# One more unit's second product by two Strassen levels, the second group's experts reordered, and w2 operands made in the first five units

## The chip, the core and the metric

The kernel runs on one core of a Trainium2 chip. The metric is the device time of one execution in microseconds (us). Three executions of the kernel before took 1161.64, 1163.95 and 1164.05 us; their median is 1163.95 us. Everything is float32.

## What is computed

The reference is a blockwise linear attention followed by a mixture of four expert networks. Cut to what matters here:

```python
# q, k, v: (4, 8, 768, 64) -> attn_out of the same shape, by blocks of 64 rows
x = attn_out.transpose(0, 2, 1, 3).reshape(3072, 512)      # 3072 tokens
p = probs / (probs.sum(-1, keepdims=True) + 1e-9)          # (3072, 4)
for e in range(4):
    h = np.maximum(x @ w1[e], 0.0)                         # first product, 512 -> 1024
    out += p[:, e:e + 1] * (h @ w2[e])                     # second product, 1024 -> 512
```

## The kernel before

**Units.** The 3072 tokens are cut into three groups of 1024, and a unit is one group with one expert: `units` (line 122) lists twelve of them. Group 0 takes the experts in the order 0, 1, 2, 3, group 1 likewise, and group 2 (`LAST`) in the order 2, 3, 0, 1. The main loop (line 1631) has an iteration `at` for each unit. In iteration `at` TensorE (PE) does the second product of unit `at` and, woven between, the first product of unit `at + 1`. An iteration has seven steps `i`, one for each of the seven Strassen products of the outer level, and each step has eight slots `x`; there are thus 56 slots in an iteration. `now[0]` counts slots, and all planning on the host side is done in slots. The program is written out in full from this plan, so the order on each engine is fixed when the kernel is built.

**Products.** The first product of all units but the first runs by two Strassen levels (`first_product`, line 993; matmuls at line 1017): 7 x 7 small products of two matmuls each. Its weights come ready made from DRAM: for each outer product a tile `ws_in` of 896 KB (`feed`, line 927, DMA at line 930), one step before it is used, into two buffers. The second product runs in one of two ways. In units before `NEST` = 6 it has one Strassen level (`second_product`, line 1056; matmuls at 1071, q<-w2t,m in the profile): seven products of 4 x 4 matmuls. In units from `NEST` on it has two levels (`nested_product`, line 1350; matmuls at 1370, pq): 7 x 7 products of two matmuls. A matmul of 128x128 weights with 256 columns is two MATMUL records in the profile, so a step of a plain unit has 28 + 32 records and a step of a nested unit 28 + 28.

**What a nested unit needs besides.** The gates are multiplied into the hidden layer before the product (`gated`, line 857: 16 multiplications of 128x512 on POOL), outer sums of it are made on VectorE (DVE) with copies into PSUM by ScalarE (ACT) (`outer_sums`), inner sums on POOL (`inner_sums`, 28 subtractions of 128x512), and results are added up in seven tiles `sums[m]` (transposed) that are allocated from the `stage` buffers at unit `NEST`. Results of a group's plain units are added up in `acc` tiles instead. Group 1 has both: the plain part is written to DRAM (`partial`) at unit `NEST - 1` and added to the nested part in unit 8 and after (`first_result`).

**Weights of the nested units.** They are ready-made operands too (`w2_ops` in DRAM): `prepare_w2_ops(e, eased)` (line 317) loads w2 of an expert by eight DMAs, makes four totals (eight operations of 128x512) and, in `inner_w2` (line 306), for each of the seven outer products four sums of 128x256, all on POOL, and stores them by six DMAs a product, 42 for an expert (line 315). With `eased` its tiles are from the pool of 42 `small` tiles, otherwise from the seven `stage` buffers. Experts 2 and 3 are made from unit 4 on and experts 0 and 1 from unit 6 on (`PREPARED`, line 1630). `prepare_w1(e)` makes the first product's operands the same way, by four loads and three stores a product, 21 for an expert (lines 218 to 220); `prepare_w2(e)` the sums for the one-level product.

**Chores.** These preparations are lists of small steps in `chores`. `pump` (line 185) is called once a slot and starts the next chore when the planned time of the one before is over: a chore's POOL time in slots, times `PACE` (1.0 in group 0, 1.4 in group 1), and at least 7 slots once `spare` is set at unit `NEST`. Stores are put off (`store`) until the planned end of the sums. `until(what)` runs chores at once until `what` is made.

**Attention of the later groups.** Groups 1 and 2 get their attention while the units before run. `BEGIN` (line 794) gives the slot of a group's first chunk of 128 tokens and the spacing of the eight chunks: (24, 13) for group 1, (152, 16) for group 2. A chunk's loads go out 10 and 6 slots ahead. Group 2 reads q and k in a transposed order that 128 small DMAs of 32 KB, DRAM to DRAM, bring about first (`bring_across`, line 435, DMAs at 441); `trickle` issues them one by one, in every second slot (`if x % 2`, line 1717), and `load_more` issues at once what a chunk still lacks.

**Queues.** Nearly every DMA is issued by SyncE (SP), in program order: `ws_in`, the small ones, attention's loads, the stores of chores. An instruction that waits there holds back all that follow. PE, DVE, ACT and POOL are in order as well.

Of the kernel before, what the change touches and what calls it, by code (L numbers as in the profile page):

```python
# [21 lines left out]
def kernel(  # L22
# [33 lines left out]
    E, DM, F = moe_w1.shape  # L56
# [6 lines left out]
    CPG = 8  # L63
    G = CPG * C
    NG = NTOK // G
# [23 lines left out]
    def bank(tag, name):  # L89
        return ps.tile([P, W], FP32, name=name, tag=tag)  # L90
# [28 lines left out]


    LAST = NG - 1
    units = [(g, e) for g in range(NG) for e in ((2, 3, 0, 1) if g == LAST else range(E))]
    unit_of = {u: x for x, u in enumerate(units)}
    NEST = 2 * E - 2
    FINAL = len(units) - 1

    def token(g, half, x):
# [45 lines left out]
    chores, queue, late, results, made = [], [], [], [], set()  # L173
# [32 lines left out]
    def until(what):  # L206
        while what not in made:
            pump(force=True)
# [582 lines left out]
        ))  # L791

    FILL = {1: 18, 2: 43}
    BEGIN = {1: (24, 13), 2: (8 * 19, 16)}
    steps = []

    def attention(g):
# [258 lines left out]
    def second_product(g, e, m, banks):  # L1056

        def part(sj, s):
            i, j = ADD[m]
            t = f"q{sj}" + ("1" if m in ("M1", "M6", "M5", "M3") else "2")  # L1060
            fresh = m in ("M1", "M2", "M7")
            if fresh and s == 0:
                banks[t] = bank(t, t)
            p = banks[t]
            first = True
            for uu in range(2):
                h = hid[g, e, uu, sj]
                while A_OF[m] not in h:
                    rest(force=True)
                for c in range(2):  # L1070
                    nc.tensor.matmul(  # L1071
                        out=p[:, s * DH:(s + 1) * DH],
                        lhsT=h[A_OF[m]][:, c * 256 + s * P:c * 256 + (s + 1) * P],
                        rhs=fed2[g, e, m][uu][:, c], start=(fresh and s == 0 and first), stop=True,
                        skip_group_check=True,
                    )
                    first = False
            n = g * CPG + sj * 4 + i * 2 + s
            if n not in acc:
                acc[n] = acc_tile("acc"), set()  # L1080
            a, begun = acc[n]
            o, x, w = a[:, j * DH:(j + 1) * DH], p[:, s * DH:(s + 1) * DH], gate[:, n, e:e + 1]
            if e == 0 and j not in begun:
                vector(DH, True)
                nc.vector.tensor_scalar(out=o, in0=x, scalar1=w, scalar2=None, op0=ALU.mult)
                begun.add(j)
            else:
                vector(DH, True)
                nc.vector.scalar_tensor_tensor(out=o, in0=x, scalar=w, in1=o, op0=ALU.mult, op1=ALU.add)  # L1089
            if unit_of[g, e] in (E - 1, NEST - 1) and m in ("M2", "M6", "M5", "M3"):  # L1090
                to = rows[n] if g == 0 else partial[n % CPG * P:(n % CPG + 1) * P]
                results.append(lambda: nc.sync.dma_start(out=to[:, j * DH:(j + 1) * DH], in_=o))

        def done():
            del fed2[g, e, m]
            if m in ("M4", "M5", "M3"):
                for uu in range(2):
                    for sj in range(2):
                        del hid[g, e, uu, sj][A_OF[m]]

        return [lambda sj=sj, s=s: part(sj, s) for s in range(2) for sj in (1, 0)] + [done]


# [523 lines left out]
        attention(g)  # L1627
    PACE = 1.0, 1.4, 1.0
    first_steps = first_result()
    PREPARED = {NEST - 2: (2, 3), NEST: (0, 1)}  # L1630
    for at, (g, e) in enumerate(units):
        if at == 0:
            chores.extend(prepare_w2(2) + prepare_w1(3) + prepare_w2(3) + prepare_w1(0))
        ahead = units[at + 1] if at + 1 < len(units) else None
        nested, nests = at >= NEST, ahead and at + 1 >= NEST
        if at in PREPARED:
            for x in PREPARED[at]:
                chores.extend(prepare_w2_ops(x, nested))
        if at == NEST:
            spare.append(True)  # L1640
        if at == NEST - 1:
            forget()
        blocks, banks = {}, {}
        for i in range(7):
            if fill2:
                feed2(*fill2.pop(0))
            if not nested:
                later_operands(g, e, SEQ2[i])
            if nested or (nests and i == 6):
                for _ in range(2 if ahead else 16 if i == 0 else 4 if i > 1 else 0):  # L1650
                    if fill3:
                        feed3(*fill3.pop(0))
            if nests and i == 2:
                nc.scalar.dma_start(
                    out=gate_bc, in_=gate_rows[ahead[0] - 1, :, ahead[1]].partition_broadcast(P),
                )
            if nested:
                pair = (at * 7 + i) % 2 if ahead else i % 3
                b = nested_product(at, SEQ3[i], (("q01", "q02"), ("q11", "q12"), ("g1", "g3"))[pair])
                if i < 6 and (at, SEQ3[i + 1]) != PLAIN:  # L1660
                    inner_sums(at, SEQ3[i + 1])
            else:
                b = second_product(g, e, SEQ2[i], banks)
            if nests and i == 6:
                inner_sums(at + 1, SEQ3[0], nested)
                if at + 1 == EARLY[0]:
                    inner_sums(*EARLY, True)
            a = []
            if ahead:
                a = first_product(*ahead, SEQ[i], blocks, ("g1", "g3"))  # L1670
            if nested and (at, SEQ3[i]) == END:
                b[6:6] = [lambda: (give("M4", 1, ("s0", "s1"), (1,)), turn_end(1, "q11"))]
                b[5:5] = [lambda: (give("M4", 0, ("s0", "s1"), (1,)), turn_end(0, "q12"))]
            if not ahead:
                order = [[], b[0:2], [], b[2:4], [], b[4:6], [], b[6:]]
            elif nested:
                order = [b[0:2], a[0:2], b[2:4], a[2:4], b[4:6], a[4:6], b[6:8], a[6:8]]
            else:
                order = [b[0:1], a[0:2], b[1:2], a[2:4], b[2:3], a[4:6], b[3:5], a[6:8]]
            turned_back = list(after_last.get(SEQ3[i], ())) if nested and not ahead else []  # L1680
            for x, part in enumerate(order):
                for f in part:
                    if f:
                        f()
                now[0] += 1
                if (at - 2 * E + 1, i, x) in first_steps:
                    first_steps.pop((at - 2 * E + 1, i, x))()
                if joins:
                    joined()
                elif (ahead or x % 2 == 0 and x + i) and not (nests and i == 6 and x == 7):  # L1690
                    if nested or nests:
                        rest()
                    else:
                        took = False
                        for of in (lately, background, own_sums):
                            if of and (not took or fits() or of is background and len(of) > 1):
                                take(of)
                                took = True
                if nested or nests:
                    take(aside)  # L1700
                    if own_sums and fits():
                        take(own_sums)
                if ending and fits():
                    end_first()
                if nested and ahead and x in (1, 3) and fill3:
                    feed3(*fill3.pop(0))
                if turned_back and x > 0:
                    for y in turned_back.pop(0):
                        if SEQ3[i] == END[1]:
                            give(*y[:2], ("s0", "s1"), *y[2:])  # L1710
                        else:
                            give_across(*y)
                if x == (4 if nested else 0) and at * 7 + i >= 6 and fill:
                    feed(*fill.pop(0))
                while steps and (at * 7 + i) * 8 + x == steps[0][0]:
                    steps.pop(0)[1]()
                if x % 2:
                    trickle()
                for h in range(1, NG):
                    if x == 3 and 0 <= at * 7 + i - FILL[h] < 7:  # L1720
                        x_fill(h, SEQ[at * 7 + i - FILL[h]])
                pump(PACE[g])
# [30 lines left out]
```

## Time and profile before

| what | value |
|---|---|
| median of three runs | 1163.95 us (1161.64 to 1164.05) |
| profiled execution, first to last instruction | 1164.6 us (no other time is given for it) |
| PE busy with matmuls | 1149.6 us, 99% |
| DVE, POOL, ACT busy | 810.8, 748.3, 306.2 us (70%, 64%, 26%) |
| matmuls L1017 pg (first product) | 1960 records, 472.0 us |
| matmuls L1071 q (second product, one level) | 1344 records, 318.7 us |
| matmuls L1370 pq<-acc,w2t (second product, two levels, the largest of its groups) | 576 records, 141.9 us |
| DMA | 270.63 MB, mean 232 GB/s |

The iterations of the main loop begin at these times, read from the first matmul of line 1017 that belongs to each: 92, 193, 299, 397, 497, 596, 688, 773, 858, 946 and 1030 us; the last one, at = 11, begins at about 1115 us. Before 92 us lie group 0's attention and its first unit's first product. A view by windows gives the busy time of each engine between two times, with the number of records in brackets, the granted TensorE clock (1.00 is full), the mean busy share of the 16 DMA engines and what they moved. The chain of waits lists what ended last, followed back from the end: a start, a length, the engine and the group it was in, and how many records.

### The profile page before, as it was taken

Reading aid. Unit: us, or ns where it says so; the run is one execution under the profiler, and the core shown is the slowest. Engines: PE = TensorE matmul, PEld = TensorE weight load, DVE = VectorE, ACT = ScalarE, POOL = GpSimd, SP = SyncE. Lnnn points to the kernel's source line nnn. Section 1 sums busy time; section 2 is a strip of 40 time slices with the busy share of each in tenths; the row PEclk is TensorE's granted clock in tenths of the full one; section 3 lists DMA queues with packets and bytes.
Section 4 is the critical chain, followed back from the end, with each engine's and each line's share of the span. In section 5 each row is a group of like instructions: output and inputs, shape, how many; then the busy total and the mean of one; then the engine's idle time right before and its main releaser. Section 6 shows DMA issues by size and latency. Waiting matters only on the chain.

```text
span 1164.6 us, 21683 instructions
## 1 busy us (share of the span) xinstructions
PE 1149.6 (99%) x8039; PEld 997.4 (86%) x8039; DVE 810.8 (70%) x1483; ACT 306.2 (26%) x618; POOL 748.3 (64%) x720
## 2 busy tenths in 40 slices
PE   8899999999999999999999999999999999999998
PEld 7788888888888888888888888888888888888887
DVE  4576896477478757747946775688875677777785
ACT  4312122112201211221221243342343341341232
POOL 2747427456754862243646395897995898995894
PEclk9999999999999999999999999999999999999999
DMA  8883668999999797787969557676668877876542
GB/s 191 213 277 119 182 190 255 311 297 284 314 301 298 258 315 204 205 261 240 291 204 281 187 190 227 213 225 216 212 222 261 244 230 227 277 225 212 172 190 73
DMA packets 291705, 270.63 MB, mean 232 GB/s; under 512 B 139600, under 2 KB 239504, under 8 KB 291600
## 3 DMA queue, kind: packets, MB, share of 16 engines
q1 hardware_dynamic: 278848, 265.36, 74.1%
q10 hardware_dynamic: 12752, 3.89, 1.5%
q8 instruction: 64, 1.05, 0.4%
q14 instruction: 41, 0.34, 0.1%
HBM read 191.55 MB, written 81.82 MB: 235 GB/s over the span
## 4 chain that ended last, share of the span: by engine, by line
PE 93%; DVE 4%; DMA 1%; issue 1%; ACT 0%; ACTq 0%; DVEq 0%
PE pg L1017 39%; PE q L1071 24%; PE pq L1370 19%; PE pM L1473 3%; PE pc L1473 2%; DVE m L102 2%; PE sp L676 1%; PE op L730 1%; DMA ws_in<-w_ops 1%; PE op L748 1%; PE sp L683 1%; DVE sums L102 1%; PE qp L646 1%; PE kp L646 1%; DVE hT L102 0%
## 5 line engine op out<-in xcount | busy, mean ns | idle before, releaser
L1017 PE MATMUL pg<-xs,ws_in 128*128 128x256 f32 x1960 | 472.0, 381 | 2.3 <-DMA ws_in<-w_ops 1.2
L1017 PEld LDWEIGHTS pg<-xs,ws_in 128*128 128x128 f32 x1960 | 369.5, 190 | 56.5 <-DVE m L102 4.6
L102 DVE TENSOR_TENSOR m<-pg,m 128x512 f32<-128x512 f32 x451 | 307.1, 687 | 124.6 <-PE pg L1017 112.8
L1071 PE MATMUL q<-w2t,m 128*128 128x256 f32 x1344 | 318.7, 380 | 0.5 <-DVE m L102 0.5
L1071 PEld LDWEIGHTS q<-w2t,m 128*128 128x128 f32 x1344 | 254.1, 190 | 35.8 <-DVE m L102 1.2
L102 POOL TENSOR_TENSOR m<-m,decay 128x512 f32<-128x512 f32 x96 | 121.0, 1282 | 75.2 <-ACT m L1029 58.0
L1029 ACT ACTIVATE m<-m 128x512 f32<-128x512 f32 x132 | 83.0, 630 | 244.4 <-DVE m L102 241.0
L1370 PE MATMUL pq<-acc,w2t 128*128 128x256 f32 x576 | 141.9, 379 | 0.2 <-DVE sums L102 0.2
L102 DVE TENSOR_TENSOR sums<-pq,sums 128x256 f32<-128x256 f32 x223 | 92.7, 421 | 59.2 <-PE pq L1370 47.8
L1089 DVE SCALAR_TENSOR_TENSOR acc<-q,gate,acc 128x256 f32<-128x256 f32 x136 | 65.4, 481 | 87.5 <-PE q L1071 86.6
L1370 PEld LDWEIGHTS pq<-acc,w2t 128*128 128x128 f32 x576 | 109.2, 190 | 15.7 <-POOL w2o L102 0.5
L102 DVE TENSOR_TENSOR m<-m,m 128x512 f32<-128x512 f32 x136 | 112.9, 830 | 4.2 <-ACT m L1029 4.2
L1025 ACT COPY m<-pg 128x512 f32<-128x512 f32 x88 | 51.5, 585 | 161.7 <-PE pg L1017 158.7
L102 POOL TENSOR_TENSOR acc<-hT,acc 128x512 f32<-128x512 f32 x48 | 61.3, 1276 | 5.2 <-PE pq L1370 1.8
L102 POOL TENSOR_TENSOR to<-xc 128x256 f32<-128x256 f32 x16 | 12.6, 785 | 79.6 <-DVE xc L102 47.1
L102 POOL TENSOR_TENSOR acc<-hT,hT 128x512 f32<-128x512 f32 x48 | 60.7, 1282 | 3.9 <-PE pq L1370 3.9
L1370 PE MATMUL pq<-hT,w2t 128*128 128x256 f32 x240 | 61.6, 379 | 0.0
L102 POOL TENSOR_TENSOR xs<-xs 128x256 f32<-128x256 f32 x40 | 30.4, 761 | 47.0 <-DMA xs<-x_blocks 33.3
L102 POOL TENSOR_TENSOR kn<-kn,decay 128x512 f32<-128x512 f32 x16 | 18.1, 1133 | 63.2 <-PE kp L646 27.6
L949 ACT COPY up<-m 128x512 f32<-128x512 f32 x48 | 27.8, 589 | 101.6 <-DVE m L102 101.4
L881 ACT COPY hp<-m 128x512 f32<-128x512 f32 x72 | 41.6, 589 | 37.5 <-DVE hT L102 20.3
L1370 PEld LDWEIGHTS pq<-hT,w2t 128*128 128x128 f32 x240 | 45.6, 190 | 6.2
(140 smaller groups left out, 1371.0 us busy)
## 6 DMA issues: line engine op xcount, KB each, us to landing
ws_in<-w_ops SPq DMA_DIRECT2D x70, 896.0 KB, 6.9
w2t<-w_ops SPq DMA_DIRECT2D x108, 256.0 KB, 3.7
w2b<-in_moe_w_dram SPq DMA_DIRECT2D x56, 256.0 KB, 6.1
w_ops<-ops SPq DMA_DIRECT2D x28, 512.0 KB, 4.7
w2t<-w_sums SPq DMA_DIRECT2D x48, 256.0 KB, 3.7
w2t<-in_moe_w_dram SPq DMA_DIRECT2D x36, 256.0 KB, 3.9
w_sums<-w2o SPq DMA_DIRECT2D x16, 512.0 KB, 5.4
xs<-x_blocks SPq DMA_DIRECT2D x28, 256.0 KB, 4.5
```

The costliest lines, as they stand in the source:

```text
L102: eng.tensor_tensor(out=o, in0=a, in1=b, op=op)
L646: nc.tensor.transpose(out=x[:, ac * C:(ac + 1) * C], in_=y[:, 2 * ac:2 * ac + 2].rearrange("p r d -> p (r d)"), identity=ident[:],)
L676: nc.tensor.matmul(out=sp[r][half[x], ac * BL:(ac + 1) * BL], lhsT=hc(kT)[half[r], ac, blk[x]], rhs=hc(qT)[half[r], ac, blk[x]], start=(ac ...
L881: nc.scalar.copy(out=there[x][:], in_=blk[at][:])
L949: nc.scalar.copy(out=there[at][:], in_=a[at][:])
L1017: nc.tensor.matmul(out=p[:, j * 256:(j + 1) * 256], lhsT=ws[i][:, j * P:(j + 1) * P], rhs=xs[i], start=(fresh and j == 0), stop=True, skip ...
L1025: nc.scalar.copy(out=new[at][:], in_=p[:])
L1029: nc.scalar.activation(out=new[at][:], in_=new[at][:], func=AF.Relu)
L1071: nc.tensor.matmul(out=p[:, s * DH:(s + 1) * DH], lhsT=h[A_OF[m]][:, c * 256 + s * P:c * 256 + (s + 1) * P], rhs=fed2[g, e, m][uu][:, c], ...
L1089: nc.vector.scalar_tensor_tensor(out=o, in0=x, scalar=w, in1=o, op0=ALU.mult, op1=ALU.add)
L1370: nc.tensor.matmul(out=p[:, 0:256], lhsT=fed3[e, m, x // 2][:, x % 2, c * P:(c + 1) * P], rhs=b[B_OF[i]][:, c * 256:(c + 1) * 256], start= ...
L1473: nc.tensor.matmul(out=p[:, s * 256:(s + 1) * 256], lhsT=a[c][:, f:f + P], rhs=b[:, c, j * 256:(j + 1) * 256], start=(s == 0 and c == 0 an ...
```

## The change

The unit before the nested ones becomes nested too (`NEST` is 5). Group 1 takes its experts in the order 1, 2, 3, 0, so that its one plain unit is expert 1, and expert 0's first-product operands are needed at unit 7 instead of unit 4. The w2 operands of experts 2 and 3 go into the chores ahead of expert 0's w1 operands, those of expert 0 after them, all from unit 0 on; only expert 1's are left for unit `NEST`, which begins by running chores until expert 0's w1 operands are made. Attention of group 1 is spaced by 12 slots instead of 13; that of group 2 begins at slot 24 + 12 * 8 = 120 instead of 152, spaced by 12 instead of 16, so that it ends before unit 4. The small DMAs go out in every slot instead of every second one from step 8 on (the second step of unit 1).

```diff
-    units = [(g, e) for g in range(NG) for e in ((2, 3, 0, 1) if g == LAST else range(E))]
+    ORDER = {0: (0, 1, 2, 3), 1: (1, 2, 3, 0), LAST: (2, 3, 0, 1)}
+    units = [(g, e) for g in range(NG) for e in ORDER[g]]
...
-    NEST = 2 * E - 2
+    NEST = 2 * E - 3
...
-    BEGIN = {1: (24, 13), 2: (8 * 19, 16)}
+    BEGIN = {1: (24, 12), 2: (24 + 12 * CPG, 12)}
...
-            if e == 0 and j not in begun:
+            if e == ORDER[g][0] and j not in begun:
...
-    PREPARED = {NEST - 2: (2, 3), NEST: (0, 1)}
     for at, (g, e) in enumerate(units):
         if at == 0:
-            chores.extend(prepare_w2(2) + prepare_w1(3) + prepare_w2(3) + prepare_w1(0))
+            chores.extend(prepare_w2(2) + prepare_w1(3) + prepare_w2(3))
+            for x in (2, 3):
+                chores.extend(prepare_w2_ops(x, False))
+            chores.extend(prepare_w1(0))
+            chores.extend(prepare_w2_ops(0, True))
...
-        if at in PREPARED:
-            for x in PREPARED[at]:
-                chores.extend(prepare_w2_ops(x, nested))
         if at == NEST:
+            until(("w1", 0, "M4"))
+            chores.extend(prepare_w2_ops(1, True))
             spare.append(True)
...
-                if x % 2:
+                if x % 2 or at * 7 + i >= 8:
                     trickle()
```

## The prediction

> **What bounds the kernel now.** First the busy shares, then the chain of waits, then the stages by windows, then SP's timeline. The page and its chain:
>
> ```profile
> PEclk9999999999999999999999999999999999999999
> DMA  8883668999999797787969557676668877876542
> ...
> PE 93%; DVE 4%; DMA 1%; issue 1%; ACT 0%; ACTq 0%; DVEq 0%
> ```
>
> PE at full clock is the chain for 93%, in every slice. DMA is near full in slices 7 to 14 (about 200 to 440 us) and lower after. The chain, step by step inside unit 6, shows the price of a matmul record:
>
> ```profile
> 698.58 1.73 PE pq L1370 x8
> 700.31 1.73 PE pg L1017 x8
> 702.03 1.73 PE pq L1370 x8
> ```
>
> Eight records take 1.73 us, 0.216 us each, in both products; the 381 ns of the groups' list are overlapping records. One step of a plain and one of a nested iteration, by windows (two records more are counted than start inside):
>
> ```profile
> 609.40:622.35 12.95, 12.95 (x62) 11.40 (x61) 4.01 (x7) 2.34 (x4) 4.28 (x5) 1.00 0.95 279
> 700.15:712.24 12.09, 12.09 (x58) 10.64 (x57) 5.65 (x10) 5.72 (x12) 7.94 (x8) 1.00 0.66 199
> ```
>
> 60 records last 12.95 us, 56 last 12.09 us, PE without a gap in both. So PE bounds iterations 1 to 10, and what counts is records removed and gaps added.
>
> **Removed: matmuls.** Unit 5's second product changes from 7 x 32 = 224 records to 7 x 28 = 196. 28 x 0.216 = 6.05 us; by the steps, 7 x (12.95 - 12.09) = 6.02 us. I take **-6.0**. All of it is on the path. Attention's matmuls are moved, not changed, and cost the same wherever they lie.
>
> **Added beside PE in unit 5 and just before.** POOL: 16 gate multiplications x 1.282 + 28 inner sums x about 1.28 = 56 us; one more gate broadcast of 512 KB. DVE: 49 additions x 0.421 + 16 outer sums x 0.68 = 31.5 us in place of 28 x 0.481 + 16 x 0.83 = 26.8 us, +5 us. ACT: 20 copies into PSUM x 0.589 = 12 us. The cover is what the iterations that are nested already show, with the same work:
>
> ```profile
> 688.00:773.00 85.00, 84.93 (x394) 74.24 (x392) 55.16 (x92) 33.65 (x73) 65.97 (x60) 1.00 0.73 232
> 773.00:858.00 85.00, 84.98 (x393) 74.58 (x394) 71.83 (x131) 27.56 (x49) 74.24 (x68) 1.00 0.71 224
> ```
>
> POOL is busy 66 and 74 of 85 us and PE loses 0.1. There POOL carried w2 operands too, which partly leave. I cost it at 0; were the cover gone, each POOL operation that a matmul waits for costs 1.28 us. The 1 us gap on the way into nesting (670 us, PE waits for two DVE additions) moves to the unit before and stays.
>
> **Moved: w2 operands.** One expert is 8 totals x 1.39 + 28 sums x 0.77 = 32.7 us of POOL, 8 loads and 42 stores. Experts 2 and 3 move from 503 to 653 us to about 350 to 490 us, directly where expert 0's w1 operands (until 426 us now) end; those follow until about 570 us, then expert 0's w2. POOL has room: 58 of 98 us in unit 2, 44 of 100 in unit 3. In slots: an expert's w2 or w1 is planned at 11 x 2.13 + 8 = 31 slots; w1 of expert 0 now ends at slot 184 (426 us); in its place stands expert 2's w2, then 31 for expert 3's w2 and 6 for sums of x that come earlier, to 221, then 31 x 1.4 = 43 for w1, to 264. The forced run at slot 280 (596 us, as now) finds it made, with 16 slots to spare; what it costs if not is a rival. The seven `sums` tiles then take stage buffers that are free. In units 6 to 9 the w2 work falls from two experts to one and a rest: less POOL, less on SP. Unit 9's start now has 3.1 us of gaps (86.18 us of PE in 88 between 858 and 946, the step at 883.6 waiting for a ws_in of 11.68 us, issued behind stores, `parked` and w2 loads). Part may go; DVE's backlog there, and SP's waits on `sums`, stay. Between 0 and -3.1, I take **-0.5**, as only four of SP's entries just ahead of that ws_in are w2 loads.
>
> **Moved: attention of group 2 and the small DMAs.** This is where the room is smallest. The four stages from unit 1 on:
>
> ```profile
> 193.00:299.00 106.00, 105.92 (x1030) 91.44 (x1028) 71.53 (x130) 21.91 (x48) 63.99 (x68) 1.00 0.93 288
> 299.00:397.00 98.00, 97.45 (x697) 84.43 (x689) 66.51 (x113) 18.20 (x38) 58.47 (x62) 1.00 0.95 301
> 397.00:497.00 100.00, 100.00 (x839) 86.47 (x838) 68.97 (x125) 17.09 (x36) 43.55 (x53) 1.00 0.80 240
> 497.00:596.00 99.00, 99.00 (x835) 85.80 (x834) 69.59 (x124) 17.67 (x40) 46.83 (x54) 1.00 0.86 262
> ```
>
> The share of the DMA engines is 0.93 and 0.95 exactly where work is put. SP's timeline for these stages has 119, 109, 109 and 107 DMAs that keep SP 87, 79, 66 and 74 us. How near the next weights are to being late shows in unit 1: the DMA below goes out 11.8 us ahead of its first matmul, and needs 6.9 us in the median.
>
> ```profile
> 226.91 0.53 SPq L930 DMA_DIRECT2D ws_in<-w_ops  x1
> ```
> ```profile
> 238.74 1.99 PE L1017 MATMUL pg<-xs,ws_in 128*128 128x256 f32 x8
> ```
>
> So some 4 to 5 us are left there; in unit 2, with SP less behind, the same DMA goes out a full step ahead (7 to 9 us left). What the change adds:
>
> Unit 1: 36 small DMAs are out by 193 us, then 29, 29 and 34 a unit. With 4 + 6 x 8 they become 52 in unit 1, 40 in unit 2, none in unit 3: +23, +11, -34. A small one keeps SP 0.6 us (its median), 0.95 in unit 1 (27.7 us for 29). With 4 loads for group 2's first chunk, unit 1 gets 27 more: 17 us at the median, 87 + 17 = 104 of 106 us. SP no longer catches up there.
>
> Unit 2: +11 small ones, three more chunks of group 2 with 11 loads, 11 stores and 4 loads for w2 in place of w1, 3 stores of x: +40 DMAs x 0.6 = 24 us, 79 + 24 = 103. A chunk's matmuls take 2.2 us in the chain (L676 0.62, L683 0.47, L730 0.62, L748 0.47), so three of them lengthen the unit to some 105. Full again. Unit 3: -34 small ones, but 50 for w2 and 3 for x more: +19, at 66 us. Unit 4 gets emptier.
>
> The gap that this makes isn't in the trace, so from both sides. Below: 0; PE waited 1.2 us for ws_in in all, and DMA engines bear more than 0.95 for a step (1.07 between 425 and 440 us, PE 15.00 of 15). Above: at 0.95 us for each entry in unit 1, and 0.73 (79 / 109) in unit 2, with 6 us between entries, 119 and 114 us of SP are wanted in 106 and 105; less the 5 us that ws_in has left, 8 + 9 = 17 us of PE waiting. I take **+2**, nearer the lower end, since unit 2's own rows (0.95, no gap) are the nearest to the new state, and 0.6 a median.
>
> The rule that speaks against it is in the Trainium skill, DMA: Bandwidth & Descriptors, section Bandwidth: transfers under 64 KB are mostly descriptor cost. Our rows agree: 32 KB land in 4.6 us, 256 KB of w2t in 3.7. The fit that the page gives in its section on the anatomy of one DMA (2.0 us + bytes / 436e3, estimate 2.1 us for 32 KB) would leave the small ones harmless: 0 in place of +2, and a sum of -6.0. By the rule, with the upper bound, the sum would be +11. The measured 4.6 stands between.
>
> DVE in unit 2 carries three chunks more, about 5 us each on 66.5 us of 98, and is ahead of PE only in bursts (2.7 us of DVE stand in the chain at 377 us, where PE lost 0.9). Between 0 and three such gaps, 2.7 us; I take **+0.5**.
>
> **Sum.** -6.0 - 0.5 + 2 + 0.5 = -4.0, against the profiled span of 1164.6: 1160.6. The page gives no time beyond the span; the span lies 0.65 above the median of the runs, 1163.95, so I put the same difference on the median: **1160.0 us**.
>
> **Rivals.** (a) *SP overfull, slower than before.* Small DMAs and w2 stores put ws_in behind its step in units 1 to 3; each late one stops PE and what is lost doesn't come back. For it: the 11.8 us above, 0.95 share, 0.95 us a small DMA. Against: no gap yet from this cause there, slack in units 3 and 4. It decides from 6.5 us of waiting on (6.0 + 0.5); at 9 to 17 us the time is 1166 to 1175, say 1169. (b) *The same, smaller:* 4 to 8 us of waiting eat the gain, 1162 to 1166, say 1163.5. (c) *Relief is fuller:* no new gaps and unit 9's 3.1 us gone, -9.1: 1154.9. (d) *The change doesn't do what it says:* chores lag, and the forced run at unit 5 pours expert 0's w1 operands on POOL ahead of the gates. Three products are 12 sums x 0.77 = 9 us, the last iteration's outer sums wait: -4 + 9, 1169.
>
> **Chances.** Forecast 0.45 (1157.5 to 1161.6), (c) 0.07, (b) 0.18, (a) 0.24, (d) 0.06. This kernel's measurement can tell 0.2% (2.3 us) from no change. Forecast and (c) are faster: 0.52; (b) within: 0.18; (a) and (d) slower: 0.30. The range leaves out half of (c) and the upper part of (a): 1156 to 1171; the forecast's own range is 1157.5 to 1161.6.
>
> **What would show it.** L1071 at 1344 - 224 = 1120 records, L1370's groups 196 more; steps of 12.09 us from unit 5 on. Unit 5's iteration 85 us, not 92. For +2: ws_in going out 10 to 12 us before its step through unit 2, PE's waits for it below 4 us in all. If units 1 to 3 are longer by more than 6.5 us over their moved attention, (a) holds. If POOL is full around 596 us and PE waits at the first steps of unit 5, (d). If unit 5's steps are not 12.09, the cover on POOL failed.

## The result and the profile after

The changed kernel takes 1190.92 us (median of four runs, 1185.02 to 1194.33), the kernel before beside it 1163.34 us. The ratio on record, which is not the quotient of these two medians (1.0237), is 1.0227 with a 95% interval of 1.0201 to 1.0253. Of all executions in this document one, of the kernel with the small DMAs at full rate in unit 0, took 4034.55 us; it is left out of that kernel's ratio. Forecast were 1160.0 us, with a range of 1156 to 1171. The profiled execution took 1193.83 us and spans 1192.0 us, 27.4 us more than the span of before. Where the program says L1017, L1071, L1370, L930 and L441 for the kernel before, the kernel after has L1018, L1072, L1371, L931 and L442.

First the page of after, its DMA row of the 40 slices and its chain of waits:

```profile
DMA  8884667889899999979786767686686967566642
...
PE 78%; DMA 8%; POOL 6%; DVE 5%; issue 2%; SPq 1%; ACT 1%; ACTq 0%; POOLq 0%; DVEq 0%
```

PE's share of the chain fell from 93% to 78%; 8% of it is DMA now. The slices are too coarse to place that, the windows are not. The first column after the stretch is its length, the second PE's busy time; the last three are the clock, the DMA share and GB/s. Here are iterations 1, 2 and 5 of after:

```profile
194.00:311.00 117.00, 110.28 (x1102) 94.32 (x1100) 73.53 (x133) 23.87 (x54) 60.38 (x65) 0.99 0.87 260
311.00:431.00 120.00, 108.12 (x960) 91.19 (x964) 74.81 (x132) 17.86 (x40) 61.84 (x68) 0.96 0.93 279
...
629.00:714.00 85.00, 84.79 (x393) 74.40 (x392) 50.91 (x88) 34.21 (x72) 70.81 (x65) 1.00 0.72 219
```

Unit 5 (629 to 714 us) is what the change was to make of it: 85 us in place of 92, with 0.2 us of gaps. Units 1 and 2 are 117 and 120 us long where they were 106 and 98; PE idles 6.7 and 11.9 us in them, and the granted clock is 0.99 and 0.96. The share of the DMA engines is 0.87 and 0.93 there, and was 0.93 and 0.95 before: it fell while PE stood, which speaks against the engines being short. The first experiment tests that. The groups of the page of after say for what PE waits (the last column):

```profile
L1018 PE MATMUL pg<-xs,ws_in 128*128 128x256 f32 x1960 | 479.5, 385 | 21.7 <-DMA ws_in<-w_ops 18.8
L1072 PE MATMUL q<-w2t,m 128*128 128x256 f32 x1120 | 267.0, 381 | 0.5 <-DVE m L102 0.5
```

And its waits between 194 and 431 us, with the sum, the number and the longest:

```profile
PE pg L1018 <- DMA ws_in<-w_ops: 16.3, 8, 4.4
```

PE waits 18.8 us for `ws_in` in the whole run (1.2 before), 16.3 us of them in eight waits in units 1 and 2. One of these steps in the chain of waits of after:

```profile
335.80 0.29 SPq L1053
...
336.18 7.50 DMA ws_in<-w_ops
...
343.82 3.61 PE pg L1018 x8
347.43 1.73 PE q L1072 x8
```

The step before began at 326.9 us, and with it the buffer came free. SP issued the DMA at 336.18, 9.3 us later; it landed after 7.50 us, and PE's step began 16.9 us after the last one. Why SP came late stands on its own timeline of after, just ahead:

```profile
328.14 0.90 SPq L219 DMA_DIRECT2D w_ops<-w1o  x1
...
330.14 1.50 SPq L442 DMA_DIRECT2D across<-in_k_dram  x2
331.69 1.28 SPq L442 DMA_DIRECT2D across<-in_q_dram  x2
333.01 0.60 SPq L219 DMA_DIRECT2D w_ops<-w1b  x1
...
334.69 1.40 SPq L1053 DMA_DIRECT2D w2t<-w_sums  x2
336.18 0.44 SPq L931 DMA_DIRECT2D ws_in<-w_ops  x1
```

Between these entries lie 0.05 to 0.1 us: SP goes from one to the next and is behind, with six stores of operands, four small DMAs and two loads ahead of `ws_in`. The transfer itself is hardly slower: from issue to landing `ws_in` takes 6.9 us in the median of either kernel, and 7.4 in unit 2 of after (6.5 before).

**The account.** The loss of an iteration is its length, from first matmul to first matmul, less its records at the price of a step without gaps (0.216 us each, attention's matmuls at the times of the prediction), so it holds what slow clock costs as well:

| iteration | 0 | 1 | 2 | 3 | 4 | 5 | 6 | 7 | 8 | 9, 10 | sum |
|---|---|---|---|---|---|---|---|---|---|---|---|
| before, us | 1.7 | 0.6 | 1.1 | 0.6 | 0.5 | 1.1 | 0.4 | 0.2 | 3.2 | 0.2 | 9.5 |
| after, us | 3.9 | 10.0 | 18.4 | 1.7 | 5.8 | 0.1 | 1.8 | 1.0 | 2.2 | 0.2 | 44.9 |

35.4 us more loss, 6.0 us fewer matmuls and an iteration 0 that begins 1.2 us earlier (90.7 us) make 28.2; measured are 27.4, and 0.8 us stays unplaced. Units 1 and 2 carry 26.7 of it.

### The profile page after: what moved, and what is told of

Same layout as the page of the kernel before. It is cut to its first block, busy times and chain, and to the rows that moved or that the text cites. A ratio compares the mean times of both kernels' runs of the same rounds, so it can differ in the third digit from the quotient of the medians.

```text
span 1192.0 us, 21838 instructions
## 1 busy us (share of the span) xinstructions
PE 1155.0 (97%) x8011; PEld 996.4 (84%) x8011; DVE 821.9 (69%) x1504; ACT 316.6 (27%) x638; POOL 802.9 (67%) x764
## 4 chain that ended last, share of the span: by engine, by line
PE 78%; DMA 8%; POOL 6%; DVE 5%; issue 2%; SPq 1%; ACT 1%; ACTq 0%; POOLq 0%; DVEq 0%
PE pg L1018 33%; PE pq L1371 20%; PE q L1072 15%; DMA ws_in<-w_ops 6%; POOL acc L102 2%; PE pM L1474 2%; POOL m L102 2%; PE pc L1474 2%; DVE m L102 2%; DVE sums L102 1%; DVE xs L102 1%; PE op L731 1%; PE sp L677 1%; POOL ops L102 1%; PE op L749 1%
## 5 line engine op out<-in xcount | busy, mean ns | idle before, releaser
L1018 PE MATMUL pg<-xs,ws_in 128*128 128x256 f32 x1960 | 479.5, 385 | 21.7 <-DMA ws_in<-w_ops 18.8
L1018 PEld LDWEIGHTS pg<-xs,ws_in 128*128 128x128 f32 x1960 | 371.6, 192 | 80.8 <-issue 15.7
L1072 PE MATMUL q<-w2t,m 128*128 128x256 f32 x1120 | 267.0, 381 | 0.5 <-DVE m L102 0.5
L1072 PEld LDWEIGHTS q<-w2t,m 128*128 128x128 f32 x1120 | 214.4, 192 | 31.1 <-DVE m L102 1.2
L102 POOL TENSOR_TENSOR m<-m,decay 128x512 f32<-128x512 f32 x112 | 141.2, 1279 | 76.7 <-ACT m L1030 66.4
L1371 PE MATMUL pq<-acc,w2t 128*128 128x256 f32 x688 | 169.5, 379 | 0.2 <-POOL m L102 0.2
L102 DVE TENSOR_TENSOR sums<-pq,sums 128x256 f32<-128x256 f32 x272 | 113.1, 420 | 72.5 <-PE pq L1371 59.9
L1371 PEld LDWEIGHTS pq<-acc,w2t 128*128 128x128 f32 x688 | 130.4, 190 | 18.8 <-issue 0.5
L102 DVE TENSOR_TENSOR m<-m,m 128x512 f32<-128x512 f32 x112 | 98.1, 876 | 7.2 <-ACT m L1030 7.2
L1090 DVE SCALAR_TENSOR_TENSOR acc<-q,gate,acc 128x256 f32<-128x256 f32 x108 | 51.8, 480 | 55.0 <-PE q L1072 54.7
L102 POOL TENSOR_TENSOR w2o<-w2b 128x512 f32<-128x512 f32 x28 | 38.9, 1411 | 55.0 <-DMA w2b<-in_moe_w_dram 17.5
L1371 PE MATMUL pq<-hT,w2t 128*128 128x256 f32 x288 | 74.0, 379 | 0.1
L102 POOL TENSOR_TENSOR xs<-xs 128x256 f32<-128x256 f32 x40 | 31.6, 790 | 44.9 <-DMA xs<-x_blocks 42.5
L1371 PEld LDWEIGHTS pq<-hT,w2t 128*128 128x128 f32 x288 | 54.6, 190 | 7.9 <-DVE sums L102 0.5
L1371 PE MATMUL pq<-m,w2t 128*128 128x256 f32 x228 | 58.5, 380 | 0.1
```

The lines of the kernel that those rows point to most:

```text
L102: eng.tensor_tensor(out=o, in0=a, in1=b, op=op)
L1018: nc.tensor.matmul(out=p[:, j * 256:(j + 1) * 256], lhsT=ws[i][:, j * P:(j + 1) * P], rhs=xs[i], start=(fresh and j == 0), stop=True, skip ...
L1072: nc.tensor.matmul(out=p[:, s * DH:(s + 1) * DH], lhsT=h[A_OF[m]][:, c * 256 + s * P:c * 256 + (s + 1) * P], rhs=fed2[g, e, m][uu][:, c], ...
L1371: nc.tensor.matmul(out=p[:, 0:256], lhsT=fed3[e, m, x // 2][:, x % 2, c * P:(c + 1) * P], rhs=b[B_OF[i]][:, c * 256:(c + 1) * 256], start= ...
```

## The experiments

Theory S: SP, which issues in order, has more entries (DMAs to issue) in a stretch than it can issue in it, so everything in its queue is late, `ws_in` with it. Rivals: E, the DMA engines themselves are full, whoever issues; W, the early work for w2 is what costs, not attention and the small DMAs. Each run has the kernel before beside it (1163.36 us in the first four, 1164.56 and 1164.61 in the others).

**Small DMAs issued by ACT.** The same DMAs in the same slots, from ACT's queue:

```diff
-                    pieces.append((b, lambda to=to, src=src: nc.sync.dma_start(
+                    pieces.append((b, lambda to=to, src=src: nc.scalar.dma_start(
```

> The changed kernel, with the 128 small DMAs (32 KB, DRAM to DRAM) issued by ACT's queue instead of SP's; the same transfers, slots and engines. Theory S (SP's issuing order is full: each entry holds SP 0.6 to 0.95 us, so ws_in goes out late, PE waits and then runs its next 3.4 us at half clock): SP gets 50 and 41 entries less in units 1 and 2, PE's waits for ws_in there fall from 16 us to under 3, no clock drop, 1156 to 1164 us. Rival E (the 16 DMA engines are full): the same bytes in the same time, PE still waits 12 us or more there, 1183 to 1193 us.

Measured: 1173.67 us, 1.0079 [1.0052, 1.0105], 17 us less than after, but above the 1156 to 1164 us expected of S (E: 1183 or more). Unit 1 loses 1.4 us instead of 10.0, with a DMA share of 0.97: the engines had room, and E falls. Unit 2 keeps 10.5, 9.0 of them in one step. Its waits between 350 and 385 us, and three steps of its chain of waits:

```profile
ACT m L1030 <- DMA across<-in_k_dram: 12.9, 1, 12.9
...
DVE m L102 <- ACT m L1030: 9.1, 1, 9.1
...
PE pg L1018 <- DVE m L102: 5.9, 1, 5.9
```

```profile
361.16 4.82 DMA w2b<-in_moe_w_dram
...
366.00 1.09 ACTq L442
...
367.13 0.64 ACT m L1030
```

PE waits for DVE, DVE for ACT, and ACT's compute for a small DMA: the instruction that issues the next one stands ahead of it in ACT's queue and, by the chain of waits, goes on (366.0 us) only when another has landed; why, the last section says. The loss was moved to another queue, at one place.

**Small DMAs at full rate in unit 0, at half rate after.**

```diff
-                if x % 2 or at * 7 + i >= 8:
+                if x % 2 or at == 0:
```

> The changed kernel, with the small DMAs in every slot of unit 0 and in every second slot after it, instead of every slot from step 8 on; all else kept. Unit 0 has a DMA share of 0.60 and an SP with room; about 28 entries move there. Theory S: unit 1 has about 28 small ones instead of 50, PE's waits in units 1 and 2 fall to 3 to 10 us, 1162 to 1174 us. Rival E: about 0.4 us of engine time for each entry moved, 10 us, 1178 to 1184 us. Rival W (the early w2 operands hold POOL and the stores): no better than 1187 us.

Measured: 1177.37 us, 1.0097 [1.0063, 1.0130], 3 us above the range expected of S and just below E's, so the time alone doesn't tell the two apart. Unit 2 loses 1.9 us, unit 1 still 6.5, and unit 3, where the last small ones now meet the stores for w2, 11.6. The loss goes where the entries go.

**Attention and small DMAs alone.** The kernel before with the new `BEGIN` and the new rate; `NEST`, expert order and w2 operands as before:

```diff
-    BEGIN = {1: (24, 13), 2: (8 * 19, 16)}
+    BEGIN = {1: (24, 12), 2: (24 + 12 * CPG, 12)}
...
-                if x % 2:
+                if x % 2 or at * 7 + i >= 8:
```

> The kernel before, with only the attention slots and the faster small DMAs of the change (units 0 to 5 one-level, order of experts and w2 operands as before). Theory S: unit 1 as in the changed kernel (27 entries more), unit 2 with 25 of its 40 entries more, so waits of 10 to 20 us and three or four clock drops: 1173 to 1185 us. Rival W: the w2 operands are the cause and this one stays within 3 us of before: 1160 to 1166 us.

Measured: 1187.93 us, 1.0199 [1.0159, 1.0239], a little above the range. Units 1 and 2 lose 8.6 and 20.1 us, as in after, without a w2 operand in them. For these two units W falls.

**Order and early w2 operands alone.** After with attention's slots, the rate and `NEST` of before:

```diff
-    NEST = 2 * E - 3
+    NEST = 2 * E - 2
...
-    BEGIN = {1: (24, 12), 2: (24 + 12 * CPG, 12)}
+    BEGIN = {1: (24, 13), 2: (8 * 19, 16)}
...
-                if x % 2 or at * 7 + i >= 8:
+                if x % 2:
```

> The changed kernel, with the nested units from 6 on as before, and attention's slots and the small DMAs' rate as before: the order of group 1 and the early w2 operands alone. Theory S: units 0 and 1 as before; unit 2 has 15 entries more, unit 3 some 50 more beside its 34 small ones, where SP waits 28 us for others now: waits of 0 to 6 us, 1162 to 1170 us. Rival W: waits as in the changed kernel, 1180 us or more.

Measured: 1193.74 us, 1.0244 [1.0204, 1.0284]. S as I had worked it out was wrong here: units 1 and 2 are whole (0.3 and 1.2 us), but units 3 and 4 lose 17.5 and 15.3. SP's timeline in unit 4 tells why, the same trouble at another place:

```profile
516.04 7.71 SPq L442 DMA_DIRECT2D across<-in_k_dram  x8
523.79 0.61 SPq L458 DMA_DIRECT2D qx<-across  x1
...
528.91 0.48 SPq L931 DMA_DIRECT2D ws_in<-w_ops  x1
```

The old schedule of the small DMAs left 35 of them for units 3 and 4; eight go out in one piece of 7.71 us when a chunk asks for them, and `ws_in`, free to go since 511 us, leaves at 528.91. The run ends where W put it, but not for W's reason: with the same w2 operands after loses 1.7 us in unit 3. So the two parts of the change seem to belong together: the early w2 operands have room where the small DMAs have left unit 3, and either part alone costs about as much as both.

**The small DMAs earlier as well.** Two kernels with `trickle` in every slot from unit 0 on, one from ACT, one from SP:

```diff
-                if x % 2 or at * 7 + i >= 8:
-                    trickle()
+                trickle()
```

> The changed kernel, with the 128 small DMAs issued by ACT in every slot from unit 0 on, so that all are out by step 14. In the run with them on ACT 12.9 us of ACT's compute waited behind one of them at 353 us (unit 2), a single gap of 9 us. Theory S (SP's order was the bound, and what is left of the loss is ACT held by those DMAs in unit 2): that gap goes, units 1 and 2 stay under 4 us of gaps together, 1161 to 1167 us. Rival L (ACT is held wherever it issues them): a gap of the same kind comes in unit 0 or 1, 1170 to 1178 us.

> The changed kernel, with the small DMAs in every slot from unit 0 on, all on SP. Theory S (entries on SP count, each stage for itself): unit 0 gets 28 more (SP was free there), unit 1 keeps its 50 or so and its 8 to 10 us of gaps, unit 2 loses its 40 and with them most of its 18 us: 1172 to 1180 us. If the gaps of unit 2 came from attention's loads or the w2 operands instead, unit 2 keeps over 12 us: 1186 us or more.

Measured from ACT: 1166.68 us (12 runs), 1.0021 [1.0011, 1.0032]; from SP: 1181.89, 1.0149 [1.0131, 1.0167]. From SP it is 2 us above the expected range, from ACT within it. On ACT the small DMAs end at 314 us, and units 1 and 2 lose only 2.6 and 2.0 us, with the DMA engines at 0.97 and 0.98; `ws_in` lands after 7.0 us in the median there, so moving the small DMAs didn't speed it up. The kernel from ACT, units 1 and 2 by windows:

```profile
194.00:300.00 106.00, 104.69 (x1025) 89.76 (x1024) 71.05 (x128) 22.73 (x53) 61.55 (x66) 1.00 0.97 296
300.00:405.00 105.00, 104.12 (x973) 89.60 (x972) 77.07 (x137) 18.94 (x42) 65.28 (x69) 1.00 0.98 307
```

This is the state that the forecast had assumed for after: full engines, PE at 0.99 in both units, clock 1.00. From SP the loss of unit 2 falls from 18.4 to 7.0 as 9 instead of 41 small ones are left in it, and unit 1 keeps 11.2, with 55 instead of 49.

**Other slots for attention, with the small ones on ACT from the start.** Two more kernels:

```diff
-    BEGIN = {1: (24, 12), 2: (24 + 12 * CPG, 12)}
+    BEGIN = {1: (24, 13), 2: (24 + 13 * CPG, 11)}
```

> As the one before, and group 1's attention spaced by 13 slots as in the kernel before, group 2's from slot 128 by 11. The 2.0 us gap at 178 us (PE waits for POOL's decay of k, behind sums of w1), which all runs with spacing 12 have and the one with 13 has not, should go: 1 to 3 us below the run before it; 1159 to 1165 us. If the gap isn't from the spacing, the same time within 1 us.

and the same with `{1: (26, 12), 2: (26 + 12 * CPG, 12)}`:

> The run with the small DMAs on ACT from unit 0 on, with attention of both groups begun two slots later ((26, 12) and (122, 12)). If the 2.0 us gap at 178 us is two pieces of POOL work meeting in one place, a shift by two slots may part them: 1 to 2 us less than that run, 1163 to 1166 us, and as good as the kernel before. If it only moves, the same within 1 us.

Measured: 1172.29 us, 1.0063 [1.0051, 1.0076], and 1166.95, 1.0027 [1.0015, 1.0038]. With 13 slots for group 1 the gaps of PE between 178 and 188 us in unit 0 go (1.5 us together, read as 2.0 in the expectation), but units 1 to 3 lose 4.8, 5.0 and 3.4 us with group 2 at 11 slots: my expectation of a gain was wrong. Two slots later the losses only move (unit 0 4.6, unit 3 2.9).

**Early w2 operands alone, small ones on ACT.** The kernel with order and early w2 operands alone, and the first experiment's edit besides, both shown above:

> The run with order and early w2 operands alone (nested from unit 6, attention and rate as before), with the small DMAs issued by ACT. Theory S: its 33 us of gaps in units 3 and 4 came from 34 small ones, w2 stores and group 2's loads together on SP; with the small ones off SP they fall below 10 us: 1164 to 1173 us. Rival W (POOL or the stores' waits hold it): 1185 us or more.

Measured: 1184.91 us, 1.0161 [1.0144, 1.0177]; the expectation was too low by 12 us. With half the rate the small DMAs are still under way in units 3 and 4, and there ACT's compute is held behind them, as in the first kernel, now twice. Its waits from 400 to 560 us:

```profile
ACT m L1030 <- DMA w2t<-w_sums: 24.1, 1, 24.1
...
ACT m L959 <- DMA qx<-across: 16.2, 1, 16.2
```

**`ws_in` on ACT, small ones left on SP.** If only `ws_in` behind SP's queue were the trouble, this would heal it:

```diff
-        nc.sync.dma_start(out=ws[:], in_=w1_ops[e, MS.index(m)])
+        nc.scalar.dma_start(out=ws[:], in_=w1_ops[e, MS.index(m)])
```

> The changed kernel, with nothing but the 70 DMAs of ws_in issued by ACT instead of SP. SP keeps all its small DMAs, stores and loads and stays as far behind. Theory S (what PE loses is ws_in standing in SP's order): the waits for ws_in in units 1 and 2 go although SP is still behind by 8 us or more; other loads may come late instead; 1165 to 1178 us. Rival E (16 DMA engines): the waits stay, 1185 us or more. Rival L (a DMA in ACT's order holds ACT's copies): new waits of DVE and PE for ACT, 1178 us or more.

The same edit was put on the kernel with `trickle` in every slot on SP, and on the one with the early w2 operands alone; their diffs are shown above:

> As the one before, with the small DMAs in every slot from unit 0 on, on SP. Theory S: unit 2 gets rid of its small ones, so what was late there besides ws_in comes in time: 0 to 6 us below the run before it, 1162 to 1175 us. Rival L: the same as the run before it.

> The run with order and early w2 operands alone, with ws_in issued by ACT. With the small ones on ACT instead it still lost 20 us, ACT held for 24 us by one of them. Theory S: with only one DMA a step on ACT the 33 us of gaps in units 3 and 4 fall below 12 us: 1165 to 1176 us. Otherwise (the stores of w2 operands wait for POOL on SP and everything behind them is late, not ws_in alone): 1182 us or more.

Measured: 1195.79 us, 1.0263 [1.0243, 1.0284]; with `trickle` in every slot besides 1181.30, 1.0163 [1.0129, 1.0198]; and with the early w2 operands alone 1192.21, 1.0238 [1.0224, 1.0252]. None is better than its counterpart with `ws_in` on SP by more than 1.6 us. The first and the third lie where the expectations put the theories that saw no help in it; the second lies 14.5 us below the first, where neither theory had it, and at its own counterpart's time. E is out since the first run. Yet PE's waits for `ws_in` do fall, from 18.8 to 5.3 us in the whole run of the first. What stops PE then is other work of the same queue. The chain of waits of the first:

```profile
258.89 7.41 DMA kn<-in_k_dram
266.32 0.56 SPq L442
...
270.65 7.73 DMA vn<-in_v_dram
278.45 0.33 ACTq L931
278.89 0.59 ACT qT L655
...
280.20 1.17 DVE m L102
```

Attention's loads of k and v are on the path, with small DMAs between them, and ACT and DVE come to their work behind them. ACT also has a trouble of its own now: an instruction just ahead of `ws_in` waits for other DMAs and holds ACT for up to 14.3 us, until a load of w2 issued by SP lands (464.8 us). So S has to be widened: not one late DMA, but the whole order on SP is late. How much of this loss is ACT's own, these runs don't tell.

**All of them by one measure.** SP's entries that start in an iteration, the time that they keep it, and that time over the iteration's length without its loss:

| kernel, unit | entries | small ones on SP | SP, us | share | loss, us |
|---|---|---|---|---|---|
| before, 1 | 118 | 29 | 81.4 | 0.77 | 0.6 |
| before, 2 | 108 | 28 | 73.4 | 0.76 | 1.1 |
| after, 1 | 136 | 49 | 93.4 | 0.87 | 10.0 |
| after, 2 | 151 | 41 | 103.5 | 1.02 | 18.4 |
| after, 3 | 128 | 0 | 74.3 | 0.74 | 1.7 |
| full rate in unit 0, unit 1 | 127 | 30 | 91.9 | 0.86 | 6.5 |
| full rate in unit 0, unit 2 | 120 | 26 | 88.5 | 0.87 | 1.9 |
| full rate in unit 0, unit 3 | 143 | 8 | 83.0 | 0.83 | 11.6 |
| attention alone, 1 | 138 | 50 | 92.6 | 0.86 | 8.6 |
| attention alone, 2 | 141 | 40 | 103.6 | 1.02 | 20.1 |
| after, 4 | 86 | 0 | 44.9 | 0.50 | 5.8 |
| w2 operands alone, 2 | 118 | 27 | 78.1 | 0.81 | 1.2 |
| w2 operands alone, 3 | 156 | 27 | 93.7 | 0.94 | 17.5 |
| w2 operands alone, 4 | 102 | 8 | 62.8 | 0.63 | 15.3 |
| from start on SP, 1 | 143 | 55 | 95.4 | 0.89 | 11.2 |
| from start on SP, 2 | 121 | 9 | 88.2 | 0.87 | 7.0 |
| from start on ACT, 1 | 91 | 0 | 46.4 | 0.43 | 2.6 |
| from start on ACT, 2 | 110 | 0 | 79.1 | 0.78 | 2.0 |

Up to a share of 0.81 these units lose at most 2.6 us, apart from two; from 0.83 on all lose 6.5 us or more, apart from one. The two are units 4, whose loss lies in their first steps, where stores from unit 3 and (with the w2 operands alone) a burst of eight small ones fill the queue; the one is unit 2 at 0.87 with 1.9 us. So the share of a whole unit is a guide, and the order within it decides. Units in which ACT is held by its own DMAs are left out: unit 2 of the first kernel loses 10.5 us at a share of 0.62.

## Why the prediction was wrong

**Right: the gain.** L1072 has 1120 records, unit 5 lasts 85 us, and its gap on the way into nesting moved a unit ahead (now at 614 us). The -6.0 us are there. POOL (71 of 85 us) held; the last of expert 0's w1 operands were stored at 609 us, 20 us before unit 5, so no forced run poured work on it, and rival (d) has no trace. The relief at unit 8, forecast at -0.5, is -1.0.

**Right: the mechanism of rival (a), and its place.** `ws_in` late behind SP in units 1 and 2. The entries that it counted are there, too: +27 and +40 forecast, +18 and +43 in the table.

**Wrong: its size.** The step that failed is "I take **+2**, nearer the lower end, since unit 2's own rows (0.95, no gap) are the nearest to the new state, and 0.6 a median". Measured are 26.7 us. Three things were mis-sized in it. First, the share of the DMA engines was taken for the measure; it fell to 0.87 and 0.93 while PE stood, and the kernel with the small DMAs on ACT from the start runs at 0.97 and 0.98. The measure was SP's own: the prediction had it at 104 of 106 and 103 of 105 us, wrote "SP no longer catches up there" and "Full again", and took next to nothing for it. Second, 0.6 us was the price of a small entry; in units 1 and 2 they take 0.76 and 0.78 (37.2 us for 49, 31.9 for 41), about midway to the 0.95 that the upper end used. Third, even the upper end of 17 us, which is close to the 16.3 us that PE waited for `ws_in`, was no bound. It left out what a wait does after it: of the 26.7 us, some 7 are PE at half clock behind four of the waits (below), and the other loads of SP's queue are as late as `ws_in`, as the runs with `ws_in` on ACT show. How much these alone cost in after was not measured.

**Not in the sum.** Unit 4, 5.3 us more, 1.0 of them the moved gap. At 546 us the next `ws_in`, whose buffer is free, leaves only at 553.78, behind six stores of w2 operands and two loads. PE waits 2.1 us for it and loses 1.8 at half clock. "Unit 4 gets emptier" was true of the unit (86 entries, before 106), not of its first steps. Unit 0, 2.2 us more: in the steps from 178 us on PE stands 1.07 us at 182.6, by the profile for DVE's `m`, and 0.45 us at 187.4 for `kn`, which POOL makes only after its sums for x, `ops` and `w1o`. No kernel with group 1's spacing of 13 has gaps there, and all with 12 have some, a move that the prediction had at no cost. Units 6 and 7: 1.4 and 0.8. DVE's +0.5 in unit 2 came about as forecast: PE stands 0.99 us there for DVE's `m` (415.7 us), and stood 0.55 us before. Of the two figures weighed from the Trainium skill's page DMA: Bandwidth & Descriptors, the rule on transfers under 64 KB (section Bandwidth; +11) lay nearer the measured +27.4 than the fit of the section on the anatomy of one DMA (-6.0), which the page gives for DMAs issued from GpSimd, not from SP. Both speak of the transfer, and what failed was the queue that issues it.

**What the forecast would have been without SP's trouble.** The kernel on ACT from the start measures it: 1166.68 us, not 1160. Its losses are 17.5 us against 9.5 of before; these 8 us, in pieces of 1 to 2 us from units 0 to 8, eat the 6 us of matmuls. No version tried beats the kernel before. One `ws_in` buffer more, or fewer and larger DMAs in place of the small ones, were not tried.

**The chances.** Slower had 0.30, rival (a) 0.24, and the range ended at 1171, above which lay only the upper part of (a). "Full again" for two stretches of an in-order queue that feeds PE should have been the likeliest case.

## What to carry to other kernels

Before work is moved earlier, count what the queue that issues in order gets in the new stage, entries times the time of one in that stage, and set it against the stage's length; here waits began above about 0.8 of it, and below that in bursts, whatever room the transfer engines had. Moving the DMAs to a second queue bought 17 of the 27 us, and 24 with earlier slots, where they were over early; where they went on, they held that engine's own work for 9 us of PE at a time. Two parts of a change that each overload the same queue may only be sound together, so a part tried alone tells little of the whole.

## What the runs showed of the hardware

**PE at half clock after a wait.** In after the granted clock falls to half for 3.4 us at 262, 344, 364, 398 and 562 us, each time about when PE goes on after a wait for `ws_in`. In the chain above the first eight records take 3.61 us where eight take 1.73 later, so that each wait costs some 1.7 us more than itself, 8.5 us in all five: 0.7% of the span, and more than all that the change gained. The kernel before has none of these between 44 us and its end, and the kernel on ACT from the start has a clock of 1.000. The five waits are 2.1 to 4.4 us long, and three of 1.0 to 1.5 us were not followed by one. The length alone doesn't decide: in the kernel from the start on SP a wait of 1.8 us (to 264.2 us) was followed by one, a wait of 2.1 us (to 361.6) was not. The stretch isn't always 3.4 us either: it is 6.8 us after the wait of 5.9 us in the first experiment's kernel. The Trainium skill, TensorE: Matmul & The Clock Gate, section Part 1: The HAM clock gate, states that after an idle window of about 3.4 us the clock passes at half rate until a busy one is over. Our stretch of 3.4 us agrees with it; but four of the five waits are shorter than such a window, so here the measured ones decide.

**The issue of a DMA isn't small here.** An entry keeps SP 0.69 us in the mean in units 1 and 2 of after, 0.59 in its unit 0, and 0.51 in unit 1 of the kernel on ACT from the start. In unit 2 of that kernel it is 0.72, though no small DMA goes through SP there; what makes an entry longer in one unit than in another was not tested. The Trainium skill, DMA: Bandwidth & Descriptors, section Issuing engines are not separate DMA queues, states that issuing from several engines saves only the issue time, which is usually small beside the transfer. For the small ones it is 0.76 us against some 4.5 of landing, and in the same slots 15 us (from the start) to 17 us (as in after) of the kernel's time hung on who issues them.

**A DMA on ACT's queue can hold ACT's compute**: the compute behind such DMAs waited 12.9, 16.2 and 24.1 us. The semaphores in the traces' records tell for what. The DMAs of SP and ACT together use eight semaphores in turn, and in the four traces followed (after, small ones on ACT, on ACT from the start, `ws_in` on ACT) none of the some 1000 DMAs in each starts before the one before it on its semaphore has landed. So at most eight are under way, and a DMA on ACT can stand until one of SP's lands. In units 1 and 2 of the first experiment's kernel 43 of ACT's 90 small ones go out within 0.12 us of such a landing. On SP in units 1 and 2 of after it is 15 of 287, with 13.7 us of waiting, and before 16.2 us: this limit isn't what made `ws_in` late there.
